# Top-k attention before two gated layers: the softmax's scale, row sums and normalisation

## The chip, the cores and the metric

The kernel runs on one core of a Trainium2 chip, as one program. The metric is the device time of one execution in microseconds. In the profile, PE is TensorE, PEld its weight loads, DVE VectorE, ACT ScalarE, POOL GpSimd and SP SyncE, whose queue issues the DMAs.

## What is computed

Attention over 4 batches of 8 heads, 576 rows of 64 columns, where each row keeps its 32 largest scores; then a layer with SiLU gates behind an RMS norm, then one with sigmoid gates, both 512 to 1536 to 512 wide, over 2304 rows:

```python
scores = scale * np.matmul(q, k.transpose(0, 1, 3, 2))
kth = np.partition(scores, -top_k, axis=-1)[..., -top_k:-top_k + 1]
scores = np.where(scores >= kth, scores, -1000000000.0)
attn = np.exp(scores - np.max(scores, axis=-1, keepdims=True))
attn = attn / (np.sum(attn, axis=-1, keepdims=True) + 1e-09)
out = np.matmul(attn, v)
# rows of all heads side by side, then
xn = x / rms * rms_g;  x = (silu(xn @ w_gate) * (xn @ w_val)) @ w_out
x = (sigmoid(x @ w_gate2) * (x @ w_val2)) @ w_out2
```

## The kernel before

**Products in two parts.** Every float32 operand is scaled by a power of two and split into a high part and a rest in float16. A product is the sum of high by high, high by rest and rest by high, accumulated in float32 by PE.

**Order of the work.** The kernel does not issue its instructions in the order of the program text. A Scheduler (L122) takes them down with a priority, estimates each one's cost by fixed formulas (`cost`, L182) and issues them by a list schedule (`order`, L209): each engine takes the most urgent instruction whose operands and buffers are ready in that model. So each engine's queue is fixed when the kernel is built, and a change of instructions makes a new order everywhere. All instructions are issued by L317, which is why every row below has that line, and the tiles' names tell them apart.

**Stages.** DVE, ACT and POOL prepare the weights of both layers (`prep_piece`, L416) beside the attention of the first rows. The attention runs through 16 units of 128 rows with 8 heads each (`attention_full`, L659; two groups of four heads) and four groups for the last 64 rows of the heads (`attention_rest`, L676; two heads in one tile). A group of four tiles is one call of `attend4` (L631): 36 calls, 144 tiles. The two layers ("experts" below; tiles pg, pw, py, po) follow the attention unit by unit, some units behind, in the same queues.

**One tile** (`attend`, L590). PE makes 128 x 576 scores sp in PSUM (two buffers). DVE finds the 8 largest (MAX8) and strikes them out (MATCH_REPLACE8) in turn until the 32nd largest is known. ACT makes e = exp(sc * sp + nb), with nb = -sc * max from POOL (L599). DVE multiplies e by the mask sp >= 32nd largest (L609) and writes the row sum through accum_out into ss. e is then multiplied by PSC = 8192, on ACT for the first tile of a group and on POOL for the others (L612). ACT rounds it to float16 (ph, high part), POOL subtracts for the rest of it (L618, L619), a DMA transposes ph into pt. PE multiplies pt by v into pv (L622): for five blocks of 128 rows of pt, the high parts, by [v high | v rest], 128 columns, and for four blocks, the rests, by v high, 64 columns. pv has one PSUM buffer for four tiles.

**The end of a group** (L645). f = 1 / ((ss + 1e-9) * PSC), times the inverse scales of v (three DVE operations on [128, 4]); ACT copies the columns of pv that came from v's rest into tl; DVE adds the others; POOL multiplies by f into x, from which the first layer's norm (`enter1`, L780) goes on. sc, the four tiles' scale of the scores, is one DVE operation at the group's start (L638).

**v** (`prep_kv`, L531): vt holds, for each of 2 heads and 5 blocks, 64 columns of high parts and 64 of rests.

Of the kernel before, what the change touches and what calls it, by code (L numbers as in the profile page):

```python
# [9 lines left out]
F32 = mybir.dt.float32  # L10
F16 = mybir.dt.float16
# [10 lines left out]
# Bits of a float m seen as an integer: RSQ - bits / 2 are those of m ** -0.5 within 4%.  # L22
RSQ = 1597463007
# A part scaled by pow2_scale lies below 1.05 * 2 ** 15, inside the range of float16.
TOP = 15
PSC = 8192.0

# How far (ns) the queue of transfers may run ahead of the DMA engines, how long an array that has
# idled runs at half its clock, and what is added to each instruction's latency.
# [3 lines left out]
# Priorities of the list schedule, in TAU per tile of 128 rows: layer 1 and 2's weights (the first  # L33
# piece, and a step), the first rows' loads, the experts' products (the lag of the first behind
# the attention, its growth and its limit), and the lead of their vector work.
# [6 lines left out]
# Units of 128 rows that share a load of layer 2's weights, and the piece of them (of 9) whose  # L42
# preparation the first load waits for, as both want the same buffers.
# [4 lines left out]
class _View:  # L48
    """A tile, or a view of it, that stands for the real one until its instructions are issued."""
# [45 lines left out]
class _Pool:  # L95
# [3 lines left out]
    def tile(self, shape, dtype, name, tag=None, bufs=None, lane=None):  # L99
        """Tiles of a tag get its buffers in the order of the program, within a lane."""  # L100
        key = tag or name
        s = self.sched
        t = _Tile(self, (shape, dtype, f"{name}_{len(s.tiles)}", key, bufs), (id(self), key), lane)
        s.tiles.append(t)
        s.rings.setdefault(t.key, {"bufs": bufs or self.default, "lanes": {}})["lanes"].setdefault(lane, []).append(t)
        shadow = s.shadow.dram_tensor(f"t{len(s.tiles)}", list(shape), dtype).ap()
        return _View(t, shadow, [], [])
# [14 lines left out]
class Scheduler:  # L122
    """Takes down the instructions of the kernel in the order of the program and issues them in that
    of a list schedule: each engine takes the most urgent instruction whose operands and buffers
    are there. Tile adds the waits."""
# [16 lines left out]
    @contextmanager  # L142
    def group(self):
        """The instructions inside, of one engine, are issued together."""
        self.open = []
        yield
        self.open = None

    def after(self, x):
        """The next instruction comes after the first that wrote x's tile."""  # L150
        self.first = x.tile.uses[0][1]
# [30 lines left out]
    def cost(self, eng, method, args, kw, writes, reads):  # L182
        """Time on the engine, and from then until the result is there (ns)."""
# [18 lines left out]
        # DMA: time on the queue, then that of the transfer.  # L202
# [6 lines left out]
    def order(self):  # L209
# [37 lines left out]
        while len(out) < len(self.ops):  # L247
# [21 lines left out]
            if op.eng == "tensor":  # L269
                # The clock of an array that has idled runs at half its rate for a while.  # L270
# [50 lines left out]
def topk_attention_moe_kernel(  # L321
# [14 lines left out]
    """Every float32 product runs as a sum of float16 products: an operand is scaled by a power of  # L336
    two (from its norm, on the chip) and split into a high part and a rest, which together hold its
    24 bits; TensorE adds the products of the parts in float32."""
# [4 lines left out]
    NF = S // P  # full tiles of a head's rows  # L343
    R = S - NF * P  # rows of the rest
# [38 lines left out]
    def pow2_scale(m, n, name, pl=None, out=None):  # L383
        """The power of two s with sqrt(m) * s in about 2 ** 14 .. 2 ** 15, and 1 / s."""
# [8 lines left out]
    # ---------------------------------------------------------------- weights  # L393
    def load_f32(dst, src, on_pool):
        """dst [P, 512] = src in float32, from the words of float64 (24 bits of them)."""
# [10 lines left out]
        if on_pool:  # L406
            # The three lowest bits of d are clear: an integer sum is exact.
# [8 lines left out]
    def prep_piece(w, kind, j, g, s, i, place):  # L416
        """Piece j of w, times g along its rows, split into float16 parts. Its scale, from the
        norm of four columns or of the piece, and the scale's inverse go to s and i [P, 1]; place(c) [P, 1024]
        takes [hi | lo] of 128 rows, and their float32 before that."""
        fs = []  # L420
        ps = ps_m.tile([P, P], F32, name="wps", tag="mm", lane="wps")
        for c in range(CPJ):
# [4 lines left out]
            if g is None:  # L427
                # Sums of products of columns, from their upper halves: none exceeds the largest square sum.
# [60 lines left out]
    def consts1():  # L489
        """Scales of layer 1: C[j] = U / (s_o s_v) and 1 / U, U the least s_g s_v s_o / 2 ** 45."""  # L490
# [23 lines left out]
    # -------------------------------------------------------------- attention  # L514
    def prep_kv(b, p, sc):
# [24 lines left out]
        vt = kvp.tile([P, 2, NF + 1, 2, D], F16, name="vt", bufs=5)  # L540
        vrf = vr.rearrange("p h j d -> p (h j) d")
        vtf = vt.rearrange("p h j a d -> p (h j) a d")
        s, i = scale_of(vr.rearrange("p h j d -> p (h j d)"), vt.rearrange("p h j a d -> p (h j a d)"), sc, p, 1)
        nc.scalar.activation(vtf[:, :, 0], vrf, AF.Copy, scale=s)
        nc.scalar.activation(vrf, vrf, AF.Copy, scale=s)
        nc.gpsimd.tensor_tensor(out=vtf[:, :, 1], in0=vrf, in1=vtf[:, :, 0], op=ALU.subtract)
        return kt, vt

    def scale_of(x, junk, sc, p, a):
        """The scale of a pair's rows x, from their norm; it and its inverse go to sc[0], sc[1]."""  # L550
# [6 lines left out]
    def prep_q(loads):  # L557
        """Rows of four heads, or of the four pairs' rests: [hi; lo] and [lo; hi], transposed."""
# [18 lines left out]
    def kcols(kt, x, j):  # L577
        """Columns of head x of a pair: the full tiles (j = 0) or the rest."""
# [11 lines left out]
    def attend(parts, sc, ssum, pv, n):  # L590
        """One tile of 128 rows. parts: (rows, qa, qb, kt, vt, x); pv: where its [hi | lo] goes."""
# [7 lines left out]
        nc.gpsimd.tensor_scalar(nb, m8[:, 0:1], sc, -1.0, op0=ALU.mult, op1=ALU.mult)  # L599
# [4 lines left out]
        for it in range(TOPK // 8 - 1):  # L604
# [4 lines left out]
        nc.vector.scalar_tensor_tensor(  # L609
            out=e, in0=sp, scalar=m8[:, 7:8], in1=e, op0=ALU.is_ge, op1=ALU.mult, accum_out=ssum  # L610
        )
        if n == 0:  # L612
            nc.scalar.activation(e, e, AF.Copy, scale=PSC)
        else:
            nc.gpsimd.tensor_scalar(e, e, PSC, 1.0, op0=ALU.mult, op1=ALU.mult)
# [6 lines left out]
        with E.group():  # L622
            for rows, qa, qb, kt, vt, x in parts:
                for c in range(2 * NF + 1):
                    if c <= NF:
                        vc, o = vt[:, x, c].rearrange("p a d -> p (a d)"), pv[rows]
                    else:
                        vc, o = vt[:, x, c - NF - 1, 0], pv[rows, 0:D]
                    nc.tensor.matmul(o, lhsT=pt[:, c, rows], rhs=vc, start=c == 0, stop=c == 2 * NF)

    def attend4(tiles, qi, ki, vi, dst):  # L631
        """Four tiles; their outputs, normalised, to dst [P, 4, D]. ki, vi [P, a, b], a * b = 4:
        the inverse scales of their keys and values."""
        a, b = ki.shadow.shape[1:]
        pv = ps_v.tile([P, 4, P], F32, name="pv")
        ss = tiny.tile([P, 4], F32, name="ss")
        sc = tiny.tile([P, 4], F32, name="sc")
        nc.vector.tensor_scalar(  # L638
            sc.rearrange("p (a b) -> p a b", a=a), ki, qi, 1.0 / math.sqrt(D), op0=ALU.mult, op1=ALU.mult
        )  # L640
        base = E.prio
        for n, parts in enumerate(tiles):
            E.prio = base + TAU / 8 * n
            attend(parts, sc[:, n : n + 1], ss[:, n : n + 1], pv[:, n], n)
        f = tiny.tile([P, 4], F32, name="f")  # L645
        nc.vector.tensor_scalar(f, ss, 1e-9, PSC, op0=ALU.add, op1=ALU.mult)
        nc.vector.reciprocal(f, f)
        f3 = f.rearrange("p (a b) -> p a b", a=a)
        nc.vector.tensor_tensor(out=f3, in0=f3, in1=vi, op=ALU.mult)
        tl = xp.tile([P, 4, D], F32, name="tl", bufs=1)  # L650
        nc.scalar.activation(tl, pv[:, :, D:P], AF.Copy)
        nc.vector.tensor_tensor(out=tl, in0=pv[:, :, 0:D], in1=tl, op=ALU.add)
        nc.gpsimd.tensor_tensor(
            out=dst, in0=tl, in1=f[:, :, None].to_broadcast([P, 4, D]), op=ALU.mult
# [4 lines left out]
    def attention_full(b, t, kv, sc):  # L659
        x = xp.tile([P, H, D], F32, name="x")  # L660
        base = E.prio
        for a in range(2):
# [9 lines left out]
            ki, vi = (sc[1][:, 2 * a : 2 * a + 2, y : y + 1].bitcast(F32).to_broadcast([P, 2, 2]) for y in range(2))  # L672
            attend4(tiles, qi, ki, vi, x[:, 4 * a : 4 * a + 4])
        return x

    def attention_rest(b, kv, sc, x):  # L676
# [20 lines left out]
        ki, vi = (sc[1][:, :, y : y + 1].bitcast(F32) for y in range(2))  # L697
        attend4(tiles, qi, ki, vi, xr)
# [4 lines left out]
    # -------------------------------------------------------------------- moe  # L703
    def split_rows(src, a, name):
        """src * a [P, 512] as [hi | lo] in float16, transposed: [P, 8, P]."""
# [9 lines left out]
    def product(ps, lt, w, start=True, stop=True):  # L715
        """ps += lt^T w: lt [P, 8, P] four high parts and four rests, w four of [P, 1024], [hi | lo]."""
# [9 lines left out]
    def gated(xt, wg, wv, gsc, vsc, silu, name, bufs, last=False):  # L726
        """sigmoid(gate) * val (times gate) for 512 columns, split and transposed; gsc is half the
        scale of gate, and sigmoid(x) = (1 + tanh(x / 2)) / 2. In the last rows, which nothing
# [233 lines left out]
```

## Time and profile before

| | us |
|---|---|
| median of 3 runs (1314.38 to 1319.67) | 1317.35 |
| the profiled execution, from first to last instruction | 1315.8 |
| DVE busy in it (2695 instructions) | 1152.1 |
| PE busy (6344 matmuls) | 1069.4 |
| POOL busy (1100) | 970.7 |
| ACT busy (1513) | 855.6 |

The page gives busy times, a chain of waits followed back from the last instruction, and groups of like instructions; the trace behind it gives the same for any stretch. Ends of matmuls are modelled: a burst's true pace is read from the starts. A duration can overlap that of the next instruction on the same engine, for which the starts help too.

### The profile page before, as it was taken

The numbers are of one execution on the slowest core, as the hardware profiler recorded it, in microseconds if no ns is written. First come the engines' busy times: TensorE is split into PE (matmuls) and PEld (weight loads), VectorE is DVE, ScalarE is ACT, GpSimd is POOL, SyncE is SP. The second block draws the span as 40 slices with busy tenths as digits, with TensorE's granted clock in tenths as the row PEclk, the third lists the DMA queues.
The fourth block names the chain that finished last, engine by engine and source line by source line (L and its number), as shares of the span: only waits on it lengthen the run. The fifth ranks groups of instructions, "written<-read, shape, count | busy, mean of one in ns | idle before, by whom it ended". The sixth has DMA issues, their size and how long they took to land.

```text
span 1315.8 us, 20791 instructions
## 1 busy us (share of the span) xinstructions
PE 1069.4 (81%) x6344; PEld 531.3 (40%) x6344; DVE 1152.1 (88%) x2695; ACT 855.6 (65%) x1513; POOL 970.7 (74%) x1100
## 2 busy tenths in 40 slices
PE   2222323758789999989999999999999999999998
PEld 1112212324334444444444444445544444444443
DVE  7999999999998899999999999998899999990012
ACT  6756665757576867657786766777875666654521
POOL 4877888878686968877797877878877787865510
PEclk9999555869899999999999999999999999999999
DMA  8655577975799898889899878899987998687475
GB/s 285 188 182 155 135 226 217 250 175 138 142 201 207 174 212 193 190 171 215 182 207 219 189 171 182 195 188 196 224 186 152 205 194 183 143 190 184 119 188 165
DMA packets 454016, 247.29 MB, mean 188 GB/s; under 512 B 411152, under 2 KB 419344, under 8 KB 453904
## 3 DMA queue, kind: packets, MB, share of 16 engines
q1 hardware_dynamic: 453904, 245.96, 80.5%
q8 instruction: 50, 0.82, 0.3%
q14 instruction: 62, 0.51, 0.1%
HBM read 137.37 MB, written 14.16 MB: 115 GB/s over the span
## 4 chain that ended last, share of the span: by engine, by line
DVE 48%; PE 23%; POOL 9%; issue 7%; DMA 6%; ACT 5%; SPq 1%; POOLq 0%; ACTq 0%; DVEq 0%
DVE m L317 14%; DVE w L317 12%; PE pw L317 8%; PE pg L317 7%; DVE wh L317 5%; DVE e L317 5%; PE po L317 4%; DMA pt<-ph 3%; POOL ph L317 2%; POOL sg L317 2%; DVE w1v L317 2%; DVE w1o L317 2%; DVE w1g L317 2%; DVE f L317 2%; PE py L317 2%
## 5 line engine op out<-in xcount | busy, mean ns | idle before, releaser
L317 DVE MAX8 m<-w 128x8 f32<-128x576 f32 x432 | 319.1, 750 | 3.3
L317 POOL TENSOR_TENSOR ph<-e,ph 128x512 f16<-128x512 f32 (+1 forms) x288 | 210.8, 753 | 54.2 <-ACT ph L317 53.6
L317 DVE MATCH_REPLACE8 w<-m,w 128x576 f32<-128x576 f32 x288 | 212.9, 740 | 0.0
L317 PEld LDWEIGHTS <-yt 128*128 128x128 f16 x1296 | 124.6, 99 | 150.8 <-issue 10.5
L317 PEld LDWEIGHTS <-xt 128*128 128x128 f16 x1296 | 123.1, 99 | 144.4 <-issue 8.6
L317 PEld LDWEIGHTS <-ht 128*128 128x128 f16 x1296 | 123.0, 98 | 142.4 <-issue 3.7
L317 ACT ACTIVATE e<-sp,nb,sc 128x576 f32<-128x576 f32 x144 | 118.3, 825 | 72.8 <-DVE w L317 19.4
L317 PE MATMUL pg<-wl,yt 128*128 128x512 f16 x648 | 150.5, 382 | 5.8 <-DMA yt<-sn 3.4
L317 PE MATMUL pg<-w1g,xt 128*128 128x512 f16 x648 | 151.9, 385 | 2.9 <-ACT g L317 1.8
L317 PE MATMUL pw<-wl,yt 128*128 128x512 f16 x648 | 152.5, 386 | 1.1 <-DVE p2t L317 0.9
L317 PE MATMUL py<-w1o,ht 128*128 128x512 f16 x648 | 151.1, 383 | 0.9 <-DMA ht<-hn 0.9
L317 PE MATMUL pw<-w1v,xt 128*128 128x512 f16 x648 | 148.7, 379 | 0.9 <-ACT sv L317 0.6
L317 PE MATMUL sp<-kt,qt 128*128 128x512 f16 (+3 forms) x640 | 102.3, 303 | 57.0 <-DVE e L317 48.3
L317 PE MATMUL po<-wl,ht 128*128 128x512 f16 x648 | 147.9, 379 | 0.6 <-DVE p2t L317 0.4
L317 POOL TENSOR_TENSOR sg<-sg,sv 128x512 f32<-128x512 f32 x102 | 130.5, 1279 | 20.4 <-ACT sv L317 19.3
L317 PE MATMUL pv<-vt,pt 128*128 128x128 f16 (+3 forms) x1440 | 92.8, 217 | 48.8 <-DMA pt<-ph 45.3
L317 POOL TENSOR_TENSOR hn<-sg,hn 128x512 f16<-128x512 f32 x102 | 119.6, 1173 | 17.2 <-ACT hn L317 17.0
L317 ACT ACTIVATE ph<-e 128x576 f16<-128x576 f32 x144 | 97.4, 678 | 52.8 <-POOL e L317 52.2
L317 DVE SCALAR_TENSOR_TENSOR e<-sp,m,e 128x576 f32<-128x576 f32 x144 | 115.9, 806 | 6.8 <-ACT e L317 4.3
L317 DVE MAX8 m<-sp 128x8 f32<-128x576 f32 x144 | 108.4, 754 | 12.7 <-PE sp L317 12.4
L317 PEld LDWEIGHTS <-pt 128*128 128x128 f16 (+1 forms) x1440 | 82.5, 105 | 84.2 <-DMA pt<-ph 65.8
L317 DVE MATCH_REPLACE8 w<-m,sp 128x576 f32<-128x576 f32 x144 | 107.3, 745 | 0.0
(150 smaller groups left out, 1864.5 us busy)
## 6 DMA issues: line engine op xcount, KB each, us to landing
wl<-w2g SPq DMA_DIRECT2D x54, 512.0 KB, 4.5
wl<-w2v SPq DMA_DIRECT2D x54, 512.0 KB, 4.8
wl<-w2o SPq DMA_DIRECT2D x54, 512.0 KB, 4.6
raw<-in_moe_w_gate_dram SPq DMA_DIRECT2D x24, 512.0 KB, 4.5
raw<-in_moe_w_val_dram SPq DMA_DIRECT2D x24, 512.0 KB, 4.5
raw<-in_moe_w_out_dram SPq DMA_DIRECT2D x24, 512.0 KB, 4.6
qr<-in_q_dram SPq DMA_DIRECT2D x32, 128.0 KB, 2.9
kr<-in_k_dram SPq DMA_DIRECT2D x16, 256.0 KB, 3.0
```

Of the source, the lines that this page charges most:

```text
L317: getattr(eng, method)(*map(real, a), **{n: real(x) for n, x in k.items()})
```

## The change

- PSC becomes 64 and moves into the exponential: nb = -sc * max + ln 64 (nsc is -sc), so that exp gives 64 e at once. Both multiplications by PSC go.
- The mask operation on DVE loses accum_out.
- vt becomes 130 wide: 64 rests, 64 high parts, two columns of ones (a DVE memset in each of the 16 `prep_kv`). Each of the nine blocks of pt is multiplied by [v high | 1], 65 columns, so the row sum arrives in column 64 of pv; for the five blocks of high parts a second matmul of 64 columns adds the product with v's rest in place.
- sc and -sc are made by one DVE operation each on [128, 1], for each pair of heads.
- f is (sum + 1e-9 * 64) * (scale of v), read from pv, one DVE operation for each pair, then the reciprocal. tl, ACT's copy and the multiplication by the inverse scale go; one DVE operation multiplies pv by f into x.
- Comments and docstrings go.

```diff
-PSC = 8192.0
+PSC = 64.0
@@ prep_kv
-        vt = kvp.tile([P, 2, NF + 1, 2, D], F16, name="vt", bufs=5)
+        vt = kvp.tile([P, 2, NF + 1, 2 * D + 2], F16, name="vt", bufs=5)
...
-        nc.scalar.activation(vtf[:, :, 0], vrf, AF.Copy, scale=s)
+        nc.scalar.activation(vtf[:, :, D : 2 * D], vrf, AF.Copy, scale=s)
         nc.scalar.activation(vrf, vrf, AF.Copy, scale=s)
-        nc.gpsimd.tensor_tensor(out=vtf[:, :, 1], in0=vrf, in1=vtf[:, :, 0], op=ALU.subtract)
+        nc.gpsimd.tensor_tensor(out=vtf[:, :, 0:D], in0=vrf, in1=vtf[:, :, D : 2 * D], op=ALU.subtract)
+        nc.vector.memset(vtf[:, :, 2 * D : 2 * D + 2], 1.0)
@@ attend
-        nc.gpsimd.tensor_scalar(nb, m8[:, 0:1], sc, -1.0, op0=ALU.mult, op1=ALU.mult)
+        nc.gpsimd.tensor_scalar(nb, m8[:, 0:1], nsc, math.log(PSC), op0=ALU.mult, op1=ALU.add)
...
-        nc.vector.scalar_tensor_tensor(
-            out=e, in0=sp, scalar=m8[:, 7:8], in1=e, op0=ALU.is_ge, op1=ALU.mult, accum_out=ssum
-        )
-        if n == 0:
-            nc.scalar.activation(e, e, AF.Copy, scale=PSC)
-        else:
-            nc.gpsimd.tensor_scalar(e, e, PSC, 1.0, op0=ALU.mult, op1=ALU.mult)
+        nc.vector.scalar_tensor_tensor(out=e, in0=sp, scalar=m8[:, 7:8], in1=e, op0=ALU.is_ge, op1=ALU.mult)
...
                 for c in range(2 * NF + 1):
+                    vc = vt[:, x, c if c <= NF else c - NF - 1]
+                    nc.tensor.matmul(pv[rows], lhsT=pt[:, c, rows], rhs=vc[:, D : 2 * D + 1], start=c == 0, stop=c == 2 * NF)
                     if c <= NF:
-                        vc, o = vt[:, x, c].rearrange("p a d -> p (a d)"), pv[rows]
-                    else:
-                        vc, o = vt[:, x, c - NF - 1, 0], pv[rows, 0:D]
-                    nc.tensor.matmul(o, lhsT=pt[:, c, rows], rhs=vc, start=c == 0, stop=c == 2 * NF)
+                        nc.tensor.matmul(pv[rows, 0:D], lhsT=pt[:, c, rows], rhs=vc[:, 0:D], start=False, stop=False)
@@ attend4
-        pv = ps_v.tile([P, 4, P], F32, name="pv")
+        pairs = len({id(t[0][3]) for t in tiles})
+        each = 4 // pairs
+        pv = ps_v.tile([P, 4, D + 1], F32, name="pv")
+        scs = tiny.tile([P, 2 * pairs], F32, name="sc", tag=f"sc{pairs}")
+        for p in range(pairs):
+            ki = sc[1][:, p0 + p, 0:1].bitcast(F32)
+            for y in range(2):
+                nc.vector.tensor_scalar(
+                    scs[:, 2 * p + y : 2 * p + y + 1], ki, qi, (1.0, -1.0)[y] / math.sqrt(D), op0=ALU.mult, op1=ALU.mult
+                )
...
-        nc.vector.tensor_scalar(f, ss, 1e-9, PSC, op0=ALU.add, op1=ALU.mult)
+        for p in range(pairs):
+            nc.vector.tensor_scalar(
+                f[:, each * p : each * p + each], pv[:, each * p : each * p + each, D],
+                1e-9 * PSC, sc[0][:, p0 + p, 1:2].bitcast(F32), op0=ALU.add, op1=ALU.mult,
+            )
         nc.vector.reciprocal(f, f)
-        f3 = f.rearrange("p (a b) -> p a b", a=a)
-        nc.vector.tensor_tensor(out=f3, in0=f3, in1=vi, op=ALU.mult)
-        tl = xp.tile([P, 4, D], F32, name="tl", bufs=1)
-        nc.scalar.activation(tl, pv[:, :, D:P], AF.Copy)
-        nc.vector.tensor_tensor(out=tl, in0=pv[:, :, 0:D], in1=tl, op=ALU.add)
-        nc.gpsimd.tensor_tensor(
-            out=dst, in0=tl, in1=f[:, :, None].to_broadcast([P, 4, D]), op=ALU.mult
+        nc.vector.tensor_tensor(
+            out=dst, in0=pv[:, :, 0:D], in1=f[:, :, None].to_broadcast([P, 4, D]), op=ALU.mult
         )
```

## Rows read from the trace of the kernel before

**Rows 1.** The page's chain that ended last: shares of the span by engine.

```profile
DVE 48%; PE 23%; POOL 9%; issue 7%; DMA 6%; ACT 5%; SPq 1%; POOLq 0%; ACTq 0%; DVEq 0%
```

**Rows 2.** Busy time by stage: stretch, length, busy us (instructions), granted clock, DMA share, GB/s.

```profile
0.00:400.00 400.00, 192.09 (x1147) 106.52 (x1148) 389.09 (x844) 257.37 (x450) 303.85 (x302) 0.82 0.72 192
400.00:1170.00 770.00, 737.65 (x4522) 360.84 (x4520) 734.00 (x1786) 542.21 (x972) 612.46 (x748) 1.00 0.89 190
1170.00:1316.00 146.00, 139.69 (x676) 63.90 (x676) 29.04 (x67) 56.00 (x93) 54.44 (x52) 1.00 0.65 166
```

**Rows 3.** The same by stage for tile tl alone: DVE, ACT, POOL.

```profile
0.00:400.00 400.00, 2.85 (x7) 2.62 (x7) 4.78 (x7) 0.82 0.72 192
400.00:1170.00 770.00, 11.59 (x28) 10.51 (x28) 17.13 (x28) 1.00 0.89 190
```

**Rows 4.** Groups by shape, DVE: xcount | busy us, mean ns | idle before, releaser.

```profile
L317 DVE TENSOR_SCALAR sc<-kvi,qi 128x4 f32<-128x4 f32 x36 | 24.9, 697 | 0.1
L317 DVE TENSOR_SCALAR f<-ss 128x4 f32<-128x4 f32 x36 | 22.5, 625 | 0.0
L317 DVE TENSOR_TENSOR f<-f,kvi 128x4 f32<-128x4 f32 x36 | 21.2, 589 | 0.0
L317 DVE TENSOR_TENSOR tl<-pv,tl 128x256 f32<-128x256 f32 x36 | 14.9, 413 | 13.5 <-ACT tl L317 13.4
L317 DVE DVE_READ_ACCUMULATOR e<-sp,m,e 128x1 f32 x144 | 11.6, 81 | 0.0
```

**Rows 5.** DVE in order of time, 815 to 833 us: start us, us, operation.

```profile
815.32 0.20 DVE L317 TENSOR_SCALAR f<-ss 128x4 f32<-128x4 f32 x1
815.43 0.14 DVE L317 TENSOR_SCALAR p2t<-qn 128x1 int32<-128x1 int32 x1
...
816.16 0.15 DVE L317 RECIPROCAL f<-f 128x4 f32<-128x4 f32 x1
...
819.88 0.08 DVE L317 DVE_READ_ACCUMULATOR e<-sp,m,e 128x1 f32 x1
819.88 0.75 DVE L317 MAX8 m<-w 128x8 f32<-128x576 f32 x1
```

**Rows 6.** Groups by shape, DVE: small operations with and without a pointer operand.

```profile
L317 DVE TENSOR_SCALAR ya<-osc,ys 128x1 f32<-128x1 f32 x18 | 3.7, 203 | 0.0
...
L317 DVE TENSOR_SCALAR p2t<-kvt 128x1 int32<-128x1 int32 x32 | 4.3, 146 | 4.3 <-PE kvt L317 4.2
```

**Rows 7.** Groups by shape: what POOL and ACT lose.

```profile
L317 POOL TENSOR_SCALAR e<-e 128x576 f32<-128x576 f32 x108 | 75.0, 694 | 38.6 <-DVE e L317 27.7 <-DVE p2t L317 9.2 <-DVE qs L317 0.9
L317 ACT ACTIVATE e<-e 128x576 f32<-128x576 f32 x36 | 24.5, 680 | 31.2 <-DVE e L317 31.1
L317 POOL TENSOR_TENSOR x<-tl,f 128x256 f32<-128x256 f32 x32 | 20.1, 629 | 14.2 <-DVE tl L317 13.1 <-DVE p2t L317 0.8
L317 ACT ACTIVATE tl<-pv 128x256 f32<-128x256 f32 x36 | 13.5, 375 | 10.7 <-PE pv L317 10.6
```

**Rows 8.** Waits, 400 to 1170 us: who for whom, us in total, times, longest.

```profile
PE pv L317 <- DMA pt<-ph: 17.0, 22, 1.5
...
DVE tl L317 <- ACT tl L317: 1.6, 2, 1.1
```

**Rows 9.** PE in order of time, 700 to 740 us: start us, us, operation.

```profile
703.86 0.57 PE L317 MATMUL pv<-vt,pt 128*128 128x128 f16 x9 [0.54 <-DMA pt<-ph]
704.26 2.75 PE L317 MATMUL pg<-wl,yt 128*128 128x512 f16 x12
706.86 2.75 PE L317 MATMUL py<-w1o,ht 128*128 128x512 f16 x12
...
709.84 0.65 PE L317 MATMUL sp<-kt,qt 128*128 128x512 f16 x4
710.33 2.75 PE L317 MATMUL po<-wl,ht 128*128 128x512 f16 x12
```

**Rows 10.** Groups by shape: weight loads of pt.

```profile
L317 PEld LDWEIGHTS <-pt 128*128 128x128 f16 x1152 | 69.9, 104 | 78.1 <-DMA pt<-ph 62.3 <-issue 2.0
```

More of the change, by code (lines that the diff above doesn't have):

```diff
@@ L539, in prep_kv @@
             )
-        vt = kvp.tile([P, 2, NF + 1, 2, D], F16, name="vt", bufs=5)
+        vt = kvp.tile([P, 2, NF + 1, 2 * D + 2], F16, name="vt", bufs=5)
         vrf = vr.rearrange("p h j d -> p (h j) d")
-        vtf = vt.rearrange("p h j a d -> p (h j) a d")
-        s, i = scale_of(vr.rearrange("p h j d -> p (h j d)"), vt.rearrange("p h j a d -> p (h j a d)"), sc, p, 1)
-        nc.scalar.activation(vtf[:, :, 0], vrf, AF.Copy, scale=s)
+        vtf = vt.rearrange("p h j d -> p (h j) d")
+        s, i = scale_of(vr.rearrange("p h j d -> p (h j d)"), vt.rearrange("p h j d -> p (h j d)"), sc, p, 1)
+        nc.scalar.activation(vtf[:, :, D : 2 * D], vrf, AF.Copy, scale=s)
         nc.scalar.activation(vrf, vrf, AF.Copy, scale=s)
-        nc.gpsimd.tensor_tensor(out=vtf[:, :, 1], in0=vrf, in1=vtf[:, :, 0], op=ALU.subtract)
+        nc.gpsimd.tensor_tensor(out=vtf[:, :, 0:D], in0=vrf, in1=vtf[:, :, D : 2 * D], op=ALU.subtract)
+        nc.vector.memset(vtf[:, :, 2 * D : 2 * D + 2], 1.0)
         return kt, vt
@@ L588, in scores, with attend @@
             nc.tensor.matmul(sp[rows, cols], lhsT=qb, rhs=rhs, start=False, stop=True)
-    def attend(parts, sc, ssum, pv, n):
+    def attend(parts, sc, nsc, pv, n):
         sp = ps_s.tile([P, S], F32, name="sp")
@@ L624, in attend, with attend4 @@
                 for c in range(2 * NF + 1):
+                    vc = vt[:, x, c if c <= NF else c - NF - 1]
+                    nc.tensor.matmul(pv[rows], lhsT=pt[:, c, rows], rhs=vc[:, D : 2 * D + 1], start=c == 0, stop=c == 2 * NF)
                     if c <= NF:
-                        vc, o = vt[:, x, c].rearrange("p a d -> p (a d)"), pv[rows]
-                    else:
-                        vc, o = vt[:, x, c - NF - 1, 0], pv[rows, 0:D]
-                    nc.tensor.matmul(o, lhsT=pt[:, c, rows], rhs=vc, start=c == 0, stop=c == 2 * NF)
-    def attend4(tiles, qi, ki, vi, dst):
-        a, b = ki.shadow.shape[1:]
-        pv = ps_v.tile([P, 4, P], F32, name="pv")
[L636 to L640, printed above, removed]
+                        nc.tensor.matmul(pv[rows, 0:D], lhsT=pt[:, c, rows], rhs=vc[:, 0:D], start=False, stop=False)
+    def attend4(tiles, qi, sc, p0, dst):
+        pairs = len({id(t[0][3]) for t in tiles})
[8 more added lines that the diff above has]
+                )
         base = E.prio
@@ L643, in attend4 @@
             E.prio = base + TAU / 8 * n
-            attend(parts, sc[:, n : n + 1], ss[:, n : n + 1], pv[:, n], n)
+            p = n // each
+            attend(parts, scs[:, 2 * p : 2 * p + 1], scs[:, 2 * p + 1 : 2 * p + 2], pv[:, n], n)
         f = tiny.tile([P, 4], F32, name="f")
-        nc.vector.tensor_scalar(f, ss, 1e-9, PSC, op0=ALU.add, op1=ALU.mult)
-        nc.vector.reciprocal(f, f)
-        f3 = f.rearrange("p (a b) -> p a b", a=a)
-        nc.vector.tensor_tensor(out=f3, in0=f3, in1=vi, op=ALU.mult)
-        tl = xp.tile([P, 4, D], F32, name="tl", bufs=1)
-        nc.scalar.activation(tl, pv[:, :, D:P], AF.Copy)
-        nc.vector.tensor_tensor(out=tl, in0=pv[:, :, 0:D], in1=tl, op=ALU.add)
-        nc.gpsimd.tensor_tensor(
-            out=dst, in0=tl, in1=f[:, :, None].to_broadcast([P, 4, D]), op=ALU.mult
+        for p in range(pairs):
+            nc.vector.tensor_scalar(
+                f[:, each * p : each * p + each],
+                pv[:, each * p : each * p + each, D],
+                1e-9 * PSC,
+                sc[0][:, p0 + p, 1:2].bitcast(F32),
+                op0=ALU.add,
+                op1=ALU.mult,
+            )
+        nc.vector.reciprocal(f, f)
+        nc.vector.tensor_tensor(
+            out=dst, in0=pv[:, :, 0:D], in1=f[:, :, None].to_broadcast([P, 4, D]), op=ALU.mult
         )
@@ L671, in attention_full @@
                 tiles.append([(full, qa[:, n], qb[:, n], kt, vt, n % 2)])
-            ki, vi = (sc[1][:, 2 * a : 2 * a + 2, y : y + 1].bitcast(F32).to_broadcast([P, 2, 2]) for y in range(2))
-            attend4(tiles, qi, ki, vi, x[:, 4 * a : 4 * a + 4])
+            attend4(tiles, qi, sc, 2 * a, x[:, 4 * a : 4 * a + 4])
         return x
@@ L696, in attention_rest @@
         xr = xp.tile([P, 4, D], F32, name="xr", bufs=1)
-        ki, vi = (sc[1][:, :, y : y + 1].bitcast(F32) for y in range(2))
-        attend4(tiles, qi, ki, vi, xr)
+        attend4(tiles, qi, sc, 0, xr)
         o = R * (b % 2)
```

## The prediction

> **What bounds the kernel now.** I read first the chain of waits that ended last: it lies on DVE for 48% of the span and on PE for 23% [rows 1]. Two engines share the end, so the next view is the busy time in three stages, cut where the experts' products become dense (400 us) and where the attention's last tiles leave DVE (1170 us) [rows 2]. Before 400 us DVE is busy 389.09 of 400 us and PE 192.09, at a mean granted clock of 0.82: DVE sets the pace. From 400 to 1170 us both are nearly full, DVE 734.00 and PE 737.65 of 770 us. After 1170 us PE has 139.69 of 146 us and DVE 29.04: a tail of products alone. So a microsecond saved on DVE before 400 us moves all that follows; in the middle it is worth something only as far as PE can use it, and PE has 770 - 737.65 = 32.35 us of idle time there; in the tail it is worth nothing. Of 36 groups of four tiles (attend4, counted by DVE's addition into tl), 7 lie in the first stage and 28 in the middle [rows 3].
>
> **DVE, removed.** Three operations on [128, 4] per group: sc 24.9 us, f 22.5 us, f times the inverse scales 21.2 us, together 68.6 us in 108 instructions [rows 4]. Beyond these there are 144 reads of the accumulator, 11.6 us, which go with accum_out. These durations overlap their neighbours: the f at 815.32 takes 0.20 us, but the next instruction starts 0.11 us later, so about 0.08 us of each small operation is not queue time; and the accumulator read at 819.88 starts together with the next MAX8, so I count its 11.6 us as nothing [rows 5]. Removed: 68.6 - 108 x 0.08 = 60.0 us.
>
> **DVE, added.** sc becomes two [128, 1] operations per pair: 4 in the 32 full groups, 8 in the 4 of the rests, 160 in all. f becomes one operation per pair that reads the row sums in PSUM: 64 + 16 = 80. Both have a pointer operand. The nearest row is ya, [128, 1] with a pointer, 203 ns; without a pointer and from PSUM it is 146 ns (p2t from kvt) [rows 6]. At 203 - 80 = 123 ns, 240 x 0.123 = 29.5 us. Sixteen memsets of [128, 20] at the same price: 2.0 us. The last operation reads pv in PSUM and f in SBUF and writes 256 elements, as the addition into tl did, which it replaces: 14.9 us against 14.9 us [rows 4].
>
> **DVE, net:** -60.0 + 29.5 + 2.0 = -28.5 us. Bounds: the new operations at 146 - 80 ns give 15.8 us instead of 29.5, and with the accumulator reads counted in full the net is -54 us. If the 80 operations for f, of two elements, cost what the old f of four did (625 - 80 ns), they take 43.6 us in place of 9.8 us, and the net is +5 us. I take the 203 ns row, since 160 of the 240 have exactly its shape. By stages, in 36ths: 28.5 x 7 / 36 = 5.5 us before 400 us and 28.5 x 28 / 36 = 22.2 us in the middle.
> A single f of [128, 4] takes 0.20 us [rows 5] where their mean is 0.625 us [rows 4]: something holds them at times, and 146 and 203 ns as means of [128, 1] say that it holds those hardly. The Trainium skill's page "SBUF — State Buffer", section "Who interferes with whom", says that GpSimd and a VectorE operation with two SBUF inputs, or in a two-port mode, block each other in full. By that rule the new f, which reads PSUM, would stay at the cheap end, and the sum above with it; no row of this trace shows that shape.
>
> **POOL and ACT.** Gone are 108 multiplications by PSC on POOL (75.0 us), 36 on ACT (24.5 us), the last multiplication on POOL (20.1 us for x; the four for the rests have the same length) and the copy of tl on ACT (13.5 us) [rows 7]. Neither engine has a full stage: POOL 303.85 of 400 and 612.46 of 770 us, ACT less [rows 2]. So I count this work at nothing. What it does shorten is the path of one tile, by the 0.694 us multiplication between DVE's e and ACT's ph. Behind that path stand PE's waits for pt, 17.0 us in the middle stage, 22 waits of up to 1.5 us [rows 8]. They are part of PE's 32 us of idle time, not beside it. The scheduler counted the multiplication when it laid the order, and lays a new order without it, so I count the shorter path as what lets PE take up DVE's saving, and not a second time. The logarithm in nb replaces one immediate by another: nothing.
>
> **PE.** A tile's pv goes from nine matmuls (five of 128 columns, four of 64) to fourteen (nine of 65, five of 64): 896 columns become 905, but five weight loads are added. The burst of nine at 703.86 is followed by pg at 704.26: 0.40 us, loads included. Twelve matmuls of 512 take 706.86 - 704.26 = 2.60 us, so 0.217 us each; the four of sp (two of 512, two of 64) take 0.49 us, so one of 64 takes about (0.49 - 0.434) / 2 = 0.03 us, its load included [rows 9]. Fourteen at 0.03 us are 0.42 us: +0.02 us for a burst, with some 125 such bursts in the middle stage (28 groups of four, those of the rests doubled), 2.5 us. The other bound is that the loads don't hide: a load of pt lasts 104 ns [rows 10], so five cost up to 0.52 us a burst and 65 us in the stage. I take 2.5 us, because the four matmuls of 64 columns in today's burst already follow each other, each with a load, at 0.03 us; what no row shows is fourteen in a row.
> The Trainium skill speaks against this part: the page "TensorE: Matmul & The Clock Gate", section "Back-to-back issue gap", gives about 81 ns for each pair of load and matmul at 128 columns in a sustained stream. The trace has nine pairs in 0.40 us, 44 ns each, so it already disagrees. By the page's figure five more pairs would be an estimated 0.4 us a burst and 50 us in the stage, near the upper bound above.
>
> **The sum.** Against the profiled execution, 1315.8 us: -5.5 us before 400 us. In the middle 22.2 us of DVE meet a chain that DVE and PE hold 48 to 23, so I let 48 / 71 = 0.68 of it through: -15.1 us, inside the 32 us that PE has. PE's 2.5 us come on top: -18.1 us, span 1297.7 us. The median stands 1.5 us above the profiled span: 1299 us.
>
> **Rival 1: PE sets the middle stage.** If PE's idle time stays (it also waits for sp and for the split rows, and the order changes), only the first stage's gain is left: 1317.35 - 5.5 + 2.5 = 1314 us, no measurable change. For it: 737.65 of 770 us, and a tail that is PE alone. Against it: the chain is on DVE twice as often as on PE.
>
> **Rival 2, slower: the weight loads don't hide in a row of fourteen.** Place: the pv bursts of the middle stage. At 0.52 us for each, PE has 737.65 + 2.5 + 65 = 805 us of work in a stage of 770. With all its idle time filled, that stage grows by 35 us; with the 5.5 us of the first, 1317.35 + 35 - 5.5 = 1347 us. It decides from (32.35 + 5.5) / 125 = 0.30 us more per burst. Against it: 0.03 us for a load with its matmul today.
>
> **Rival 3, slower: pv is held longer.** Today f, its reciprocal and the scale are done before pv is read, and DVE only adds. Afterwards f, reciprocal and product all stand behind pv's last matmul, in DVE's queue, with tile-long operations between them (f at 815.32, its reciprocal at 816.16: 0.84 us) [rows 5]. Whatever is queued on DVE behind an f that waits, the next tile's MAX8 first of all, waits too, and so does the next group's first pv, as there is one pv buffer. Two such spacings are 1.7 us; ACT's copy, 0.375 us, is saved. At 1.3 us for each of 28 groups it is 36 us against the 20.6 us gained: 1317.35 - 20.6 + 2.5 + 36 = 1335 us; it decides from 0.65 us a group. Against it: in the middle stage DVE's wait for tl is 1.6 us in two waits [rows 8], so pv is nearly always there before DVE comes to it.
>
> **How the numbers follow.** Forecast 1299 us, chance 0.63; rival 1, 0.21; rival 2, 0.07; rival 3, 0.09. The low end is DVE at -54 us: -10.5 us early, and all of PE's 32 us less its 2.5 us in the middle, 1317 - 40 = 1277 us. Upward, the range takes in rival 1 and the first steps of rival 3, 1322 us, and leaves some 15 in 100 above it. A measurement of this kernel can tell 0.5% from no change, so below 1310.8 us is faster and above 1323.9 us slower: 0.63, 0.21 and 0.16.
>
> **What would show it.** In the changed kernel's profile: [128, 1] sc and [128, 2] f at about 0.2 us (0.6 us: the DVE sum is wrong); no accumulator reads; pv bursts of fourteen in about 0.42 us (0.8 us or more: rival 2); DVE waits before f on PE below some 5 us in the middle (30 us: rival 3); PE's dense stage beginning about 5 us earlier and its idle time down from 32 us to some 17 us. If DVE's busy time falls by 28 us and the span by less than 7, rival 1 holds. The prediction is wrong in kind if the new order makes a wait of its own, which no row of this trace can price.

## The result and the profile after

The changed kernel takes 1303.39 us (median of 4 runs, 1302.73 to 1306.91) against 1317.52 us: a ratio of 0.9900, 95% interval 0.9879 to 0.9921, so 14 us or 1% faster. The profiled execution takes 1301.8 us against 1315.8 us. The forecast was 1299 us, 18 us faster.

The chain that ended last, the page of the changed kernel:

```profile
PE 40%; DVE 28%; POOL 10%; DMA 9%; issue 8%; ACT 4%; SPq 1%; POOLq 0%; ACTq 0%; DVEq 0%
```

DVE held 48% of it and PE 23% [rows 1]; now PE leads. Busy time by stage (PE, PEld, DVE, ACT, POOL, each with its instructions; then the granted clock, the DMA share and GB/s), changed kernel:

```profile
0.00:400.00 400.00, 194.63 (x1314) 108.11 (x1316) 386.15 (x850) 248.19 (x432) 280.79 (x270) 0.91 0.71 189
400.00:1170.00 770.00, 748.95 (x5229) 372.30 (x5226) 716.21 (x1810) 532.86 (x935) 560.89 (x652) 1.00 0.91 195
1170.00:1302.00 132.00, 125.72 (x606) 57.13 (x604) 15.27 (x40) 45.60 (x76) 41.05 (x36) 1.00 0.62 161
```

Beside [rows 2] these three lines hold the whole difference of the two profiled executions. PE's total is the same (1069.4 and 1069.3 us, with 800 more matmuls). By 400 us PE had started 390 of the experts' matmuls before and 396 after, by 1170 us 3252 and 3311: the lead is won in the middle. What went is idle time of PE after 400 us: 32.35 + 6.31 us before, 21.05 + 6.28 us after, 11.3 us less, nearly all in the middle. The rest, 2.7 us, is PE's busy time that lies before 400 us or came out shorter; the granted clock there (the mean of its two levels, 0.50 at 1.2 GHz and 1.00 at 2.4 GHz) was 0.82 before and 0.91 after, so the two busy times are not like amounts of work. After 400 us the clock is 1.00 in both, and the changed kernel with its multiplications back (below) has 0.83 in the first stage and the same span, 1301.4 us: the clock is not behind the difference of this pair. DVE's busy time in the middle fell by 17.8 us at the same length, so DVE now idles 53.8 us there instead of 36.0 us. Where, its waits from 400 to 1170 us tell (us in total, times, longest), first before, then after:

```profile
DVE m L317 <- PE sp L317: 12.1, 15, 2.8
```

```profile
DVE m L318 <- PE sp L318: 23.4, 32, 3.5
DVE f L318 <- PE pv L318: 12.3, 13, 4.5
```

The same of PE in the changed kernel:

```profile
PE pv L318 <- DMA pt<-ph: 11.2, 13, 1.7
```

DVE waits 23.6 us longer for PE there (12.1 us became 23.4 + 12.3 us), the 1.6 us for ACT's copy [rows 8] are gone, and PE's wait for pt fell from 17.0 [rows 8] to 11.2 us. A part of DVE's saving became a wait for PE.

Groups by shape, changed kernel (xcount | busy us, mean ns | idle before, releaser):

```profile
L318 DVE TENSOR_SCALAR sc<-kvi,qi 128x1 f32<-128x1 f32 x160 | 25.8, 202 | 0.1
L318 DVE TENSOR_SCALAR f<-pv,kvs 128x2 f32<-128x2 f32 x64 | 13.4, 209 | 17.7 <-PE pv L318 17.3
L318 DVE TENSOR_TENSOR x<-pv,f 128x256 f32<-128x256 f32 x32 | 13.2, 413 | 0.1
...
L318 DVE MEMSET vt<- 128x20 f16 x16 | 1.2, 75 | 0.0
```

Against [rows 4]: sc from 697 to 202 ns, f from 625 to 209 ns (211 ns for the 16 of one column), the scale's 589 ns gone; the last product takes 413 ns, the same as the addition that it replaces. As there are 160 sc now instead of 36, sc as a whole costs what it did, 25.8 us for 24.9; the saving lies in f and its scale. PE in order of time, 700 to 740 us, changed kernel:

```profile
709.85 0.58 PE L318 MATMUL pv<-vt,pt 128*128 128x65 f16 x14
710.27 0.65 PE L318 MATMUL sp<-kt,qt 128*128 128x512 f16 x4
```

Fourteen matmuls with fourteen weight loads take 710.27 - 709.85 = 0.42 us; nine took 0.40 us [rows 9].

### The profile page after: what moved, and what is told of

Same layout as the page of the kernel before. It is cut to its first block, busy times and chain, and to the rows that moved or that the text cites. A ratio compares the mean times of both kernels' runs of the same rounds, so it can differ in the third digit from the quotient of the medians.

```text
span 1301.8 us, 22257 instructions
## 1 busy us (share of the span) xinstructions
PE 1069.3 (82%) x7144; PEld 537.5 (41%) x7144; DVE 1117.6 (86%) x2699; ACT 826.7 (63%) x1441; POOL 882.7 (68%) x956
## 4 chain that ended last, share of the span: by engine, by line
PE 40%; DVE 28%; POOL 10%; DMA 9%; issue 8%; ACT 4%; SPq 1%; POOLq 0%; ACTq 0%; DVEq 0%
PE pg L318 12%; PE pw L318 11%; DVE m L318 7%; PE po L318 7%; DVE w L318 6%; DMA pt<-ph 6%; PE py L318 5%; DVE wh L318 4%; PE pv L318 3%; POOL ph L318 3%; POOL sg L318 3%; DVE w1v L318 2%; DVE w1g L318 2%; PE sp L318 2%; DVE e L318 2%
## 5 line engine op out<-in xcount | busy, mean ns | idle before, releaser
L318 PE MATMUL py<-w1o,ht 128*128 128x512 f16 x648 | 154.3, 389 | 2.6 <-DMA ht<-hn 2.6
L318 PE MATMUL pw<-w1v,xt 128*128 128x512 f16 x648 | 152.9, 387 | 2.9 <-DVE wn L318 2.9
L318 PE MATMUL pw<-wl,yt 128*128 128x512 f16 x648 | 148.5, 379 | 3.1 <-ACT sg L318 1.7
L318 PE MATMUL pv<-vt,pt 128*128 128x65 f16 (+1 forms) x2240 | 95.2, 199 | 25.4 <-DMA pt<-ph 25.0
L318 ACT ACTIVATE sg<-pg,gsc 128x512 f32<-128x512 f32 x108 | 73.6, 681 | 66.7 <-PE pg L318 62.6
L318 PEld LDWEIGHTS <-pt 128*128 128x128 f16 (+1 forms) x2240 | 86.4, 104 | 57.5 <-DMA pt<-ph 36.9
```

What stands on the lines that cost most here:

```text
L318: getattr(eng, method)(*map(real, a), **{n: real(x) for n, x in k.items()})
```

## Experiments

**Is it the factor or the rest?** One kernel moves the factor alone, the other undoes it alone.

```diff
 # the kernel before with the factor in the bias; sc and nsc in columns
-PSC = 8192.0
+PSC = 64.0
...
-        nc.gpsimd.tensor_scalar(nb, m8[:, 0:1], sc, -1.0, op0=ALU.mult, op1=ALU.mult)
+        nc.gpsimd.tensor_scalar(nb, m8[:, 0:1], nsc, math.log(PSC), op0=ALU.mult, op1=ALU.add)
...
-        if n == 0: nc.scalar.activation(e, e, AF.Copy, scale=PSC)
-        else: nc.gpsimd.tensor_scalar(e, e, PSC, 1.0, op0=ALU.mult, op1=ALU.mult)
...
-        nc.vector.tensor_scalar(f, ss, 1e-9, PSC, op0=ALU.add, op1=ALU.mult)
+        nc.vector.tensor_scalar(f, ss, 1e-9 * PSC, 1.0, op0=ALU.add, op1=ALU.mult)
```

> The kernel before with the factor alone moved: PSC = 64 inside the exponential's bias, both multiplications by PSC gone, sc and -sc in columns as in the changed kernel (24.9 us of DVE for 25.8 us); accum_out, the old f, tl and the nine matmuls stay. Theory 1 (the gain is DVE's saving, 28 us, of which the middle stage lets some half through): DVE's load is that of before, so 1314 to 1319 us. Theory 2 (the gain is the shorter path from e to pt, with 75 us less on POOL and 24 us less on ACT): most of the 14 us comes here, 1303 to 1308 us.

```diff
 # the changed kernel with the multiplications back
-        nc.gpsimd.tensor_scalar(nb, m8[:, 0:1], nsc, math.log(PSC), op0=ALU.mult, op1=ALU.add)
+        nc.gpsimd.tensor_scalar(nb, m8[:, 0:1], nsc, 0.0, op0=ALU.mult, op1=ALU.add)
...
+        if n == 0: nc.scalar.activation(e, e, AF.Copy, scale=PSC)
+        else: nc.gpsimd.tensor_scalar(e, e, PSC, 1.0, op0=ALU.mult, op1=ALU.mult)
```

> The changed kernel with the two multiplications by PSC back (ACT for a group's first tile, POOL for the others) and no logarithm in the bias; all else as changed. Theory 1: the multiplications are hidden, 1302 to 1307 us. Theory 2: most of the gain is lost, 1312 to 1318 us.

The factor alone: 1315.66 us, ratio to the kernel before 0.9987 (0.9969 to 1.0004), no measurable change. All but the factor: 1305.59 us, 0.9912 (0.9879 to 0.9945), within the interval of the whole change. Their middle stages, the factor alone first:

```profile
400.00:1170.00 770.00, 735.85 (x4508) 362.75 (x4506) 723.29 (x1878) 526.11 (x944) 563.13 (x665) 1.00 0.91 190
```

```profile
400.00:1170.00 770.00, 748.81 (x5193) 370.67 (x5192) 712.75 (x1791) 542.68 (x955) 605.13 (x728) 1.00 0.89 193
```

In the first, POOL is as idle as in the changed kernel (563 us busy) and PE still has 34 us of idle time. In the second, POOL works 605 us, nearly as before, and PE's idle time is 21 us, as in the changed kernel. So the shorter path to pt and the multiplications taken from POOL and ACT are not where the gain is, and theory 2 falls. The second kernel is the stronger witness: orders move the kernel before by up to 15 us (below), which could hide a gain in the first, but the changed one by 4 us.

Theory 1 is not shown in full by this. The gain comes with the part that takes work from DVE, but that part also takes ACT's copy and POOL's last product and moves the row sums to PE, and no run parts these. That the second kernel gives ACT and POOL some 85 us of busy time back for 2.2 us, and that DVE waited only 1.6 us for ACT's copy [rows 8], speaks for DVE. And DVE's busy time alone is no measure of the gain: in the first kernel it fell from 1152.1 to 1135.3 us, 10.7 us of it in the middle, without a gain that can be told from none.

**What does a microsecond of DVE or of PE cost?** The first edit repeats a MAX8 of DVE in the tile's own chain, the second a matmul of PE, in either kernel:

```diff
+        if n == 0:
+            nc.vector.max(out=m8, in_=sp)
         nc.vector.max(out=m8, in_=sp)
```

> The kernel before with the first MAX8 of each group's first tile issued twice: 36 more on DVE in the tile's own chain, 0.67 to 0.75 us each, 24 to 27 us in all, 5 of it before 400 us and 19 to 21 us in the middle. Theory 1 (DVE sets the first stage and two thirds of the middle): 17 to 20 us longer, 1334 to 1338 us. If PE sets the middle stage: 5 us, 1322 us.

> The changed kernel with the same 36 second MAX8, so DVE's load is back near that of before (1117.6 + 26 us against 1152.1 us). Theory 1: the time goes back with it, 1315 to 1322 us. Theory 2 (the path): the gain stays but for the first stage, 1306 to 1309 us. If PE sets the pace of the changed kernel (its chain lies on PE for 40%), less than half of the 26 us shows, 1303 to 1314 us.

```diff
 # in product(), for pg alone
+            if twice:
+                nc.tensor.matmul(ps, lhsT=lt[:, 0], rhs=w[0][:, 0:512], start=True, stop=True)
```

> The kernel before with the first matmul of each pg issued twice: 108 more of 512 columns, 0.216 us each, 23.3 us of PE, most of it after 400 us. If DVE sets two thirds of the middle stage, PE's 32 us of idle time there take up some of it, and what falls into the tail (some 20 of the 108, 4 us) shows in full: 8 to 14 us longer, 1325 to 1331 us. If PE sets the pace: 20 to 23 us, 1338 to 1341 us.

> The changed kernel with the same 108 matmuls, 23.3 us of PE. If the change has moved the bound towards PE (idle in the middle 21 us against 32 us, the chain 40% on PE against 23%), more of it shows than in the kernel before: 15 to 23 us, 1318 to 1326 us. If DVE still sets the middle: 8 to 12 us, 1311 to 1315 us.

The 36 MAX8 are 27 us of busy time (135.6 us for 180 of them, 108.4 us for 144 in the kernel before).

| added | kernel before | changed kernel |
|---|---|---|
| DVE, 36 MAX8, 24 to 27 us | 1337.21 us, +18.8 | 1316.73 us, +13.3 |
| PE, 108 matmuls, 23.3 us | 1341.65 us, +24.4 | 1334.07 us, +30.7 |

(The kernel before took 1318.45 us beside the first pair and 1317.23 us beside the second; the changed kernel is put at 1303.39 us.) The added MAX8 take the changed kernel back to 1317 us, in the range that theory 1 gave. But the second line contradicts what I expected of PE: in the kernel before its work was to be half hidden, and all of it shows. In the changed kernel more than all shows. Both engines count in the kernel before; in the changed kernel PE counts in full and DVE for about half.

How the time came back is not what theory 1 says, though. The page of the changed kernel with the MAX8:

```profile
PE 1079.2 (82%) x7144; PEld 537.9 (41%) x7144; DVE 1127.0 (86%) x2735; ACT 828.7 (63%) x1441; POOL 888.2 (68%) x956
```

DVE is busy only 9.3 us longer than in the changed kernel, as other operations came out shorter, and 25 us less than in the kernel before. PE is busy 9.9 us longer for the same 7144 matmuls, at a granted clock of 0.95 from 400 to 500 us, where the changed kernel has 1.00. After 400 us PE's idle time is 30.6 us instead of 27.3 us. So most of the 13 us is a longer busy time of PE, and only some 3 us is idle time of PE. With the matmuls added to the changed kernel PE's busy time rises by 29.1 us (to 1098.4 us), 6 us more than the 23.3 us added, at 0.97 from 400 to 500 us. Each of these edits also lays a new order; how much of the prices is order, clock or load stays open.

**How much does an order move?** The same instructions with another constant in the scheduler, in both kernels: the added latency at 130 and 110 ns, and an earlier start of layer 2's weights.

```diff
-MARGIN = 120
+MARGIN = 130        # the second pair: 110
```

> The kernel before with 130 instead of 120 ns in the scheduler's added latency: the same instructions, another order. How far an order alone moves the time: if the 14 us of the change are work and not luck of order, within 5 us of before, 1312 to 1322 us; if an order alone is worth 10 us or more, the comparison of single kernels says little.

> The changed kernel with the same 130 ns: the same instructions, another order. Work: 1299 to 1308 us. Luck of order: outside. In its first stage the weights' preparation on DVE, 169 us before and 174 us after the change by its rows, tells whether that lengthening belongs to the change (174 us again) or to one order (some other sum).

> The kernel before with 110 ns in the scheduler's added latency: the same instructions, a third order. With 130 ns the loss of 15 us began where the last weights' preparation on DVE came 60 us later. If the order at 120 ns is a favourable one for the kernel before: 1322 to 1335 us. If 130 ns was the exception: 1313 to 1320 us.

> The changed kernel with the same 110 ns. If the change's gain is work, each order gives at least the 14 us against the same setting of the kernel before: 1302 to 1314 us, and below the run beside it by 14 us or more. If the gain is luck of order, the two lie within 5 us of each other.

```diff
-PREP2 = (0.8, 0.02)
+PREP2 = (0.7, 0.03)
```

> The kernel before with PREP2 = (0.7, 0.03): layer 2's weights begin a tenth of a unit earlier and their pieces lie further apart in priority; a fourth order. Work: 1314 to 1330 us, above the run of the changed kernel with the same setting by some 14 us or more.

> The changed kernel with PREP2 = (0.7, 0.03). Its first stage gained 1 us where 5.5 us were forecast, and its last weights were prepared 11 us later than before; if an earlier start of them gives the first stage its gain, 1296 to 1302 us; if the stage is set by DVE's whole work whatever the order, 1302 to 1306 us.

| order | before, us | changed, us | difference |
|---|---|---|---|
| as given | 1317.52 | 1303.39 | -14.1 |
| 130 ns | 1332.66 | 1305.10 | -27.6 |
| 110 ns | 1326.90 | 1303.83 | -23.1 |
| PREP2 | 1318.42 | 1301.10 | -17.3 |

The change is faster in every order, by 20.5 us in the mean, every order of the changed kernel is faster than every one of the kernel before, and the order that the kernel before had was, with PREP2's, the best of its four. Of the two outcomes named beforehand for the kernel before at 130 ns the second came: an order can be worth more than 10 us, so a single pair says little. An order alone moves the kernel before by up to 15 us, the changed one by 4 us. So the 14 us are hardly luck; if anything the shown pair undersells the change. This also qualifies the table above: an addition to the kernel before leaves its favourable order too, so some of its 18.8 and 24.4 us may be order. In the changed kernel an order moved 4 us, but the 7.4 us by which its 30.7 us exceed the matmuls are more than that. The last row's 1301.10 us (0.9882, 0.9848 to 0.9915) can't be told from the changed kernel's own 0.9900.

PE in the middle stage, the kernel before at 130 ns, at 110 ns and with PREP2, then the changed kernel likewise (busy us of 770, with all engines):

```profile
400.00:1170.00 770.00, 724.60 (x4381) 353.89 (x4380) 723.33 (x1755) 539.49 (x965) 612.69 (x739) 0.98 0.89 191
```

```profile
400.00:1170.00 770.00, 732.95 (x4476) 358.96 (x4477) 717.91 (x1782) 544.83 (x976) 614.11 (x748) 0.99 0.90 192
```

```profile
400.00:1170.00 770.00, 745.14 (x4566) 365.51 (x4565) 733.03 (x1801) 551.87 (x989) 621.24 (x758) 1.00 0.90 195
```

```profile
400.00:1170.00 770.00, 748.61 (x5210) 371.00 (x5209) 715.46 (x1812) 530.53 (x931) 558.94 (x650) 1.00 0.90 193
```

```profile
400.00:1170.00 770.00, 750.21 (x5196) 371.63 (x5195) 716.52 (x1812) 531.48 (x929) 558.15 (x650) 0.99 0.89 194
```

```profile
400.00:1170.00 770.00, 748.55 (x5193) 369.87 (x5192) 713.49 (x1806) 529.44 (x930) 556.39 (x647) 0.99 0.89 193
```

PE's idle time is 45.4, 37.1 and 24.9 us before (32.35 us in the given order), 21.4, 19.8 and 21.5 us after (21.05 us). The loss of the kernel before at 130 and 110 ns sits early in the stage. PE's matmuls into pg from 400 to 500 us (busy us and count, clock, DMA share, GB/s), the kernel before at 130 ns:

```profile
400.00:500.00 100.00, 20.36 (x74) 0.90 0.87 208
```

They are 74 there, 88 at 110 ns and 122 with PREP2, where the given order has 120 and the changed kernel 118 to 120 in all four orders. At 130 ns PE waits there for layer 2's weights, the last of which DVE prepares at 424.8 us instead of 364.7 us. The waits of that kernel from 400 to 500 us, PE's:

```profile
PE pw L317 <- DMA wl<-w2v: 3.4, 1, 3.4
...
PE pg L317 <- DMA wl<-w2g: 2.5, 1, 2.5
```

That is not the whole reason: at 110 ns the last comes at 391.2 us, with PREP2 at 390.6 us, and only the first of these two loses. Nor do these two waits, 5.9 us, make up PE's idle time from 400 to 500 us, 21.6 us against 5.2 us in the given order. The granted clock has a part: 0.90 in that stretch at 130 ns and 0.97 at 110 ns, against 1.00 in the given order and with PREP2, and the 74 matmuls took 275 ns of busy time each where the given order's 120 took 230 ns. Over the whole kernel at 130 ns PE is busy 9.9 us longer than in the given order for the same 6344 matmuls:

```profile
PE 1079.3 (81%) x6344; PEld 534.2 (40%) x6344; DVE 1147.7 (86%) x2695; ACT 854.5 (64%) x1513; POOL 975.2 (73%) x1100
```

Why the changed kernel's orders lie so much closer together stays open.

## Why the prediction held, point by point

**DVE's saving, 28.5 us.** Right in this order. The new operations came out as the row of ya said: 202 and 209 to 211 ns for the 203 ns assumed, the memsets cheaper (75 ns). DVE's busy time fell by 34.5 us. Counting for the operations that the change touches only the time that no other operation of DVE covers, they took 64.2 us before and 31.8 us after, 32.4 us less. With 130 ns, 110 ns and PREP2 they took 58.3, 52.7 and 56.3 us before and 32.7, 32.1 and 31.6 us after, so the order alone moves this saving between 20.6 and 32.4 us, and the gain does not follow it: 23.1 us with 110 ns, where the saving is smallest. The accumulator reads were rightly left out: without them DVE's busy time before is 1152.0 instead of 1152.1 us. Their queue time is small indeed: without accum_out the next MAX8 starts 0.72 us after the mask operation (1161.78 and 1162.50), with it 0.74 us (819.14 and 819.88 [rows 5]). The bound in which f keeps its old price fell. The old f took between 150 and 4033 ns; the new one, which reads PSUM, 196 to 221 ns over all 80, and sc of one column 177 to 215 ns over all 160. By the Trainium skill's page "SBUF — State Buffer", section "Who interferes with whom", a VectorE operation with at most one SBUF input, outside the two-port modes, does not contend with GpSimd. The trace agrees for the new f.

DVE in order of time around the mask operation, the kernel before from 815 to 833 us, then the changed kernel from 1160 to 1182 us:

```profile
819.14 0.81 DVE L317 SCALAR_TENSOR_TENSOR e<-sp,m,e 128x576 f32<-128x576 f32 x1
```

```profile
1161.78 0.81 DVE L318 SCALAR_TENSOR_TENSOR e<-sp,m,e 128x576 f32<-128x576 f32 x1
1162.50 0.75 DVE L318 MAX8 m<-w 128x8 f32<-128x576 f32 x1
```

**POOL and ACT at nothing.** Right within some 2 us, by the pair of kernels on the factor: a ratio of 0.9987 for it alone, and 2.2 us of the change's gain lost without it, neither clear of the measurement.

**PE at 0.02 us for a burst.** Right: 0.42 us for fourteen, and over the middle stage PE's busy time on pv went from 66.35 us for 125 bursts to 70.45 us for 127, 0.02 us more for each. Rival 2, loads that don't hide, fell: 30 ns for each pair of load and matmul. The Trainium skill's page "TensorE: Matmul & The Clock Gate", section "Back-to-back issue gap", gives some 81 ns for a pair at 128 columns in a sustained stream. The trace differs: of the nine pairs in 0.40 us four have 64 columns at about 0.03 us, which leaves an estimated 56 ns for each of the five of 128; the measurement decides.

**The first stage, -5.5 us.** Wrong in this pair. PE had issued 144 of pg's matmuls by 400 us in both kernels. DVE's operations on the weights add up to 174 us here and 169 us before, which eats most of it; with 130 ns they are 173 and 167 us, with PREP2 174 and 172 us. But with 110 ns they are 168 us in either kernel, and the first stage gains no more. Over the orders the count is 144, 156, 144 and 136 before, 144, 144, 146 and 156 after: no gain that stands out from the order.

**The middle stage, 0.68 x 22.2 = 15.1 us, less 2.5 us.** The size was right, 11.3 us of PE's idle time, and the forecast of that (from 32 to some 17 us) near the 21 us measured. The reason for the factor was not good: I took it from the chain's shares, as if the two engines took turns. These shares are a matter of the order: 48, 44, 34 and 49% on DVE and 23, 26, 30 and 24% on PE in the four orders of the kernel before, 22 and 26% with the factor alone (1315.66 us). The added work shows both engines counting for more than a share before the change, as far as order and clock let that be read. So the mechanism, DVE's saving taken up by PE in the middle, fits what was seen, but that 18 us came so near to 14 us is partly luck: the first stage's 5.5 us did not show, the factor had no ground, and another order would have given up to 27.6 us.

**Rival 1** has its place here: PE's idle time did not stay, but PE now leads the chain. By the added MAX8 a microsecond of DVE is worth about half of itself (13.3 us for 24 to 27 us); whether that holds for a further saving no run shows. **Rival 3** was half seen: DVE's wait for pv before f is 12.3 us in the middle, between the 5 us and the 30 us named. It is the wait for which the change put f behind pv in DVE's queue, with the MAX8 behind it. The last one, 11.13 us at 1179 us, stands where DVE has nothing else to do; before, tl waited 11.8 us in the same place.

**The order.** The prediction left it to one sentence, as what it could not price. At up to 15 us for the kernel before, it is as large as the effect, and a single pair of kernels would not have told the two apart. Nor did I ask how an order acts on PE's clock.

## To carry to other kernels

Small operations on [128, 4] in SBUF can cost three times those on one column or from PSUM (589 to 697 ns in the mean here against 202 to 211 ns, though the reciprocal on [128, 4] took 161 ns), so look at their mean and spread before counting them as nothing, and sum them over the whole program. A matmul of 64 columns took 0.03 us here with its weight load, as long as the matmuls followed each other, so row sums and corrections can ride on PE. In a kernel whose order comes from a list schedule, lay a few other orders of both versions before believing a difference of one per cent, and read PE's granted clock beside each.

## What the runs showed of the hardware that I had not expected

Fourteen weight loads of 128 x 128 in float16 and fourteen matmuls of 64 and 65 columns, in turn, went through in 0.42 us, and the odd width of 65 cost nothing that can be seen. A DVE memset of [128, 20] in float16 took 75 ns, less than DVE's small operations with a pointer operand (about 200 ns). The accumulator's read, 81 ns in the groups, took about 0.02 us of DVE's queue. In the kernel before at 130 ns PE had a granted clock of 0.90 from 400 to 500 us, where it idled 21.6 us, and 1.00 in the given order, where it idled 5.2 us.
